# First loads without w_in beside them, q read straight from its turn, w_out with four rows a partition, and a new order of work

## Chip, cores and metric

One core of one Trainium2 chip. The metric is the time of one execution on the device in microseconds; lower is better. Times of the kernel before are a median of three runs, beside one execution taken with the hardware profiler.

## What is computed

Gated linear attention over 4 batches, 8 heads, 768 steps and a head width of 48, and behind it a two-layer perceptron on its output.

```python
f = 1.0 / (1.0 + np.exp(-f_logit))
for t in range(S):
    state = f[:, :, t, :, None] * state + np.einsum('bhd,bhe->bhde', k[:, :, t], v[:, :, t])
    y[:, :, t] = np.einsum('bhd,bhde->bhe', q[:, :, t], state)
...
x = attn_out.transpose(0, 2, 1, 3).reshape(B * S, H * D)     # 3072 x 384
h = x @ w_in                                                 # w_in 384 x 2048
g = np.maximum(0.01 * h, h)
return g @ w_out                                             # w_out 2048 x 384
```

## The kernel before

**Units.** The sequence is cut into 6 chunks of 128 steps; a chunk of one batch is a *unit* (24 of them, unit u = 4 * chunk + batch), and two units make a pair m = u // 2 for the perceptron. For a unit, `gate_exp`, `gate_ln`, `gate_pe` and `decay_*` turn f_logit into running decays, `k_scale` and `q_scale` multiply k and q by them, `turn_pe` transposes both, `score_pe` and `mask` make the causal scores, `mix_pe` the output y, `state_pe`, `state_dve` and `state_pool` the running state, and `y_out`, `x_pe`, `x_out` bring y as x (transposed) into `xTs`. Late units use DMA transposes (`turn_dma`, `x_dma`) instead.

**The perceptron.** `up(m, g, bank)` makes 2 of the 16 blocks of 128 hidden columns for a pair (six matmuls of 256 columns, weights from `w_in_b`), `up_act(m, g, bank)` applies the leaky ReLU into `gTs`, and `down(u, half, bank)` sums 8 hidden blocks for a unit (eight matmuls of 384 columns, `w_out_b` streaming). `put` and `out_dma` store the result.

**The first quad.** Units 0 to 3 (the first chunk of all four batches) are treated together by the functions with q_ ahead of their names: time is interleaved over the partitions (partition 4 t + b holds steps 4 t to 4 t + 3 of batch b), the gates are four pairs of accumulating matmul groups (`q_gate_pe`), the scaled k and q are transposed (`q_turn_pe`) and copied out of PSUM with the columns sorted by batch (`q_turn_out`), so that the scores of one batch read contiguous columns.

**Queues.** Every engine works through its own instructions in program order, and the order is written out by hand as the long list of calls at the end of the kernel (`manual_schedule`). SP issues all loads of f, k, q and v and all stores; ACT issues four of the first twelve loads (L77 to L89); POOL issues the six loads of weights, which convert float32 to bfloat16 on the way (`load_w_in`, two halves of 1,024 columns; `load_w_out`, four groups). A load on SP or ACT waits until the load eight before it has landed. PSUM has eight banks of 2 KB a partition, and the last argument of most calls names one. `idle_pe(n, bank)` issues n matmuls on zeros.

**The start.** SP and ACT issue f, k and q of the quad; POOL builds the small constant tiles and then issues both halves of w_in, as its first loads. ACT computes exp and ln of the gates, PE runs 40 filler matmuls and then the gate matmuls, and DVE and POOL scale k, then q.

## Time and profile before

| | us |
|---|---|
| median of 3 runs (192.94 to 193.77) | 193.02 |
| the profiled execution | 192.63 |
| its span, first to last instruction | 190.8 |
| mean granted TensorE clock of it | 0.982 of full speed |

The page gives busy times of the engines, the chain of waits that ended last, and the costliest groups of instructions by line. PE is the matmul engine, PEld its weight loads, which overlap with PE; DVE, ACT and POOL are the vector, scalar and general engines, SP the one that only issues transfers. A name with a q behind it (SPq, POOLq) is that engine's sequencer. In the DMA views, q0 is the queue of POOL's loads, q1 that of SP and q10 that of ACT; a share is the time that the queue's packets took, of 16 engines, and shares of queues can add up to more than 100%. The two instructions most of the time goes to:

```profile
L412 PE MATMUL ps<-xT,w_in_b 128*128 128x256 bf16 x576 | 70.6, 273 | 0.0
L422 PE MATMUL ps<-w_out_b,gT 128*128 128x384 bf16 x384 | 68.4, 326 | 0.0
```

L412 is the matmul of `up`, L422 that of `down`. The mean duration of one (273 and 326 ns) is longer than the step between two of them, since matmuls are pipelined.

### The profile page before, as it was taken

The page shows a single profiled execution, that of the slowest core. Times are in us where ns is not written, and L with a number is a line of the kernel's source. Part 1 is how long each engine was busy: PE and PEld are TensorE (multiplying, and loading weights), DVE is VectorE, ACT ScalarE, POOL GpSimd, SP SyncE. Part 2 cuts the span into 40 slices and gives each one's busy share as a digit, 9 for nine tenths or more (in the row PEclk, how much of TensorE's full clock was granted, in tenths as well). Part 3 has the DMA queues.
Part 4 walks back from the last instruction along what each step waited for, and adds up shares of the span by engine and source line. Part 5 has one row for each costly group of instructions (what it writes and reads, how often), then busy time and mean ns, then how long its engine had stood idle before and what let it go on. Part 6 is the DMA issues. An engine that isn't in the chain of part 4 may idle for free.

```text
span 190.8 us, 4830 instructions
## 1 busy us (share of the span) xinstructions
PE 175.7 (92%) x1905; PEld 136.3 (71%) x1905; DVE 87.4 (46%) x193; ACT 124.1 (65%) x266; POOL 59.2 (31%) x109
## 2 busy tenths in 40 slices
PE   4952679999999999999999999999999999999992
PEld 2841459886679778768877787877668787776861
DVE  7001799313597557547556436894528304010000
ACT  2661176994479879967968778986458665642822
POOL 8000855620143644441532512844502500000000
PEclk9997599999999999999999999999999999999999
DMA  4999899999088989899999999972742490113202
GB/s 143 264 222 259 172 190 213 166 185 178 25 196 190 212 176 235 167 228 200 217 193 192 221 195 191 227 157 65 156 115 62 79 138 0 45 43 83 82 3 84
DMA packets 106679, 29.42 MB, mean 154 GB/s; under 512 B 97696, under 2 KB 105888, under 8 KB 106656
## 3 DMA queue, kind: packets, MB, share of 16 engines
q1 hardware_dynamic: 102656, 25.18, 62.2%
q0 software_dynamic: 2912, 3.15, 10.1%
q10 hardware_dynamic: 1088, 0.79, 1.3%
q8 instruction: 15, 0.25, 0.5%
q14 instruction: 8, 0.07, 0.1%
HBM read 25.17 MB, written 4.72 MB: 157 GB/s over the span
## 4 chain that ended last, share of the span: by engine, by line
PE 84%; DMA 9%; ACT 2%; SPq 1%; DVE 1%; issue 1%; POOL 1%; POOLq 0%; ACTq 0%
PE ps L412 33%; PE ps L422 33%; DMA qq<-in_q_dram 6%; PE ps L332 3%; PE ps L357 3%; DMA fq<-in_f_logit_dram 2%; PE ps L371 2%; PE ps L368 2%; PE ps L304 2%; PE ps L379 2%; PE ps L402 2%; SPq L69 1%; PE ps L139 1%; PE ps L223 1%; ACT kqh L145 1%
## 5 line engine op out<-in xcount | busy, mean ns | idle before, releaser
L412 PE MATMUL ps<-xT,w_in_b 128*128 128x256 bf16 x576 | 70.6, 273 | 0.0
L422 PE MATMUL ps<-w_out_b,gT 128*128 128x384 bf16 x384 | 68.4, 326 | 0.0
L417 ACT ACTIVATE gT<-ps 128x512 bf16<-128x512 f32 x96 | 56.8, 604 | 12.3 <-PE ps L412 10.2
L412 PEld LDWEIGHTS <-w_in_b 128*128 128x128 bf16 x576 | 54.3, 98 | 7.7
L422 PEld LDWEIGHTS <-gT 128*128 128x128 bf16 x384 | 36.2, 98 | 20.6
L361 DVE TENSOR_TENSOR wm<-ps,ut 128x512 bf16<-128x512 f32 x40 | 24.9, 682 | 14.7 <-ACT gT L417 10.4
L288 POOL CAST sb<-sf 64x192 bf16<-64x192 f32 x40 | 15.1, 378 | 35.9 <-PE ps L368 31.3
L145 ACT COPY osb<-ps 128x384 f32<-128x384 f32 x23 | 11.0, 480 | 20.7 <-PE ps L422 20.7
L319 DVE TENSOR_TENSOR kqh<-k_raw,em_t 128x384 bf16<-128x384 f32 x14 | 7.9, 567 | 12.9 <-ACT em_t L311 12.7
L323 POOL TENSOR_TENSOR kqh<-q_raw,a_t 128x384 bf16<-128x384 f32 x11 | 10.3, 938 | 10.4 <-issue 7.1
L393 POOL TENSOR_TENSOR sf<-sf,a_end 128x192 f32<-128x192 f32 x16 | 9.2, 576 | 13.1 <-DVE sf L388 12.6
L147 DVE CAST xn<-ps 128x384 bf16<-128x384 f32 x12 | 6.5, 554 | 12.6 <-ACT osb L145 7.8
L311 ACT ACTIVATE em_t<-ps 128x384 bf16<-128x384 f32 x20 | 9.8, 497 | 2.5 <-PE ps L307 2.5
L147 DVE COPY kqT<-ps 128x512 bf16<-128x512 bf16 x17 | 6.8, 421 | 8.6 <-PE ps L332 5.3
L298 ACT ACTIVATE lf<-f_raw 128x384 bf16<-128x384 f32 x20 | 10.5, 532 | 0.1
L145 ACT COPY kqT<-ps 128x512 bf16<-128x512 bf16 x11 | 6.3, 587 | 6.6 <-PE ps L332 3.8
L295 ACT ACTIVATE f_raw<-f_raw 128x384 f32<-128x384 f32 x20 | 10.4, 526 | 0.0
L139 PE MATMUL ps<-fill 128*128 128x256 bf16 x60 | 9.2, 317 | 1.1 <-DVE ind L129 1.1
L314 ACT ACTIVATE a_t<-ps 128x384 bf16<-128x384 f32 x20 | 9.9, 508 | 0.0
L145 ACT CAST xn<-ps 128x384 bf16<-128x384 f32 x12 | 5.8, 480 | 4.7 <-PE ps L371 2.9
L387 DVE TENSOR_TENSOR sf<-sf,ps 64x192 f32<-64x192 f32 x16 | 5.5, 342 | 7.1 <-PE ps L379 4.2
L139 PEld LDWEIGHTS <-fill 128*128 128x128 bf16 x60 | 6.7, 114 | 2.8 <-issue 1.3
(88 smaller groups left out, 194.1 us busy)
## 6 DMA issues: line engine op xcount, KB each, us to landing
v_raw<-in_v_dram SPq DMA_DIRECT2D x24, 192.0 KB, 4.0
out_dram<-osb SPq DMA_DIRECT2D x24, 192.0 KB, 2.5
f_raw<-in_f_logit_dram SPq DMA_DIRECT2D x20, 192.0 KB, 3.9
k_raw<-in_k_dram SPq DMA_DIRECT2D x20, 192.0 KB, 4.0
q_raw<-in_q_dram SPq DMA_DIRECT2D x20, 192.0 KB, 4.0
w_in_b<-in_moe_w_in_dram POOLq DMA_DIRECT2D x2, 768.0 KB, 12.2
w_out_b<-in_moe_w_out_dram POOLq DMA_DIRECT2D x4, 384.0 KB, 8.6
qq<-in_q_dram SPq DMA_DIRECT2D x4, 192.0 KB, 12.1
```

Source lines behind the costliest of these rows:

```text
L139: nc.tensor.matmul(bank(bk)[:, 0:256], fill[:, 0:128], fill[:, 0:256], start=True, stop=True)
L145: eng.copy(out=out, in_=in_)
L147: eng.tensor_copy(out=out, in_=in_)
L288: nc.gpsimd.tensor_copy(out=state_b[b][r, :, e * D:(e + 1) * D], in_=state_f[b][r])
L295: nc.scalar.activation(raw[u]["f"], raw[u]["f"], AF.Exp, scale=-1.0)
L298: nc.scalar.activation(lfs[u % R_LF][:, :, 0:D], raw[u]["f"], AF.Ln, bias=1.0)
L314: nc.scalar.activation(a_ts[u % R_EM], bank(bk)[:, 0:H * D], AF.Exp, scale=-1.0)
L323: eng.tensor_mul(qhs[u % R_KQS][:, :, 0:D], r["q"], a_ts[u % R_EM])
L361: nc.vector.tensor_mul(wms[e][u % R_WM], bank(bk).rearrange("p (i n) -> p i n", i=P2), ut[:, None, :].to_broadcast([128, P2, 128]))
L412: nc.tensor.matmul(bank(bk)[:, i * 256:(i + 1) * 256], w_in_b[:, kk, ff * 128:(ff + 1) * 128], xTs[m % R_XT][:, kk].rearrange("p a n -> p ...
L417: nc.scalar.activation(gTs[m % GBUFS][:, 2 * g:2 * g + 2].rearrange("p f a n -> p (f a n)"), bank(bk), AF.Prelu, alpha=0.01)
L422: nc.tensor.matmul(bank(bk)[:, 0:KD], gTs[u // 2 % GBUFS][:, ff, u % 2, :], w_out_b[:, ff, :], start=(ff == 0), stop=(ff == NF - 1))
```

## The change

- **Loads of the quad.** All four k loads are issued by SP; ACT issues only two of f and loads its table of functions right after.
- **w_in.** Both halves move from POOL's first work to behind `q_q_scale(G, 0, 1)`, a new one-column copy from q (`touch('q')`) and `q_k_scale(G, 1, 0)`. The copy reads q of all four batches, so it waits for the four q loads.
- **q straight.** `q_q_out` copies the turned q out of PSUM as it lies (512 contiguous columns); `q_score_pe` picks one batch's columns with a step of four elements as it streams them. k is sorted by batch as before.
- **w_out.** Partition p of group g holds rows 512 g + 4 p to 512 g + 4 p + 3, so each partition's part is one piece of 6,144 bytes of the source. For the sums to match, hidden block ff = 4 g + i of `up` is now made of the columns 512 g + 4 n + i of w_in (n = 0 to 127): the weight load reads w_in_b with a step of four elements (`w_in_p`). The first half of w_in still holds ff 0 to 7, so `up(m, g)` with g from 0 to 3 needs the first half alone.
- **Order.** The list of calls is a new one. It has the same calls of `up`, `down`, `score_pe`, `mix_pe`, `state_pe`, `turn_pe`, `x_pe`, `turn_dma` and `x_dma`; 52 filler matmuls instead of 60; and some copies and products on another engine (ACT has 18 `y_out` instead of 12, and 24 `put` instead of 23). Of the list, the diff below shows the new lines up to the second store, without the old ones.

```diff
@@ -79,11 +79,11 @@
     first_load(nc.sync, "f", 1)
     first_load(nc.scalar, "f", 3)
     first_load(nc.sync, "k", 0)
-    first_load(nc.scalar, "k", 2)
+    nc.scalar.preload_act_table_set("natural_log_exp_and_others")
     first_load(nc.sync, "k", 1)
-    first_load(nc.scalar, "k", 3)
+    first_load(nc.sync, "k", 2)
+    first_load(nc.sync, "k", 3)
     first_load(nc.sync, "q", 0)
-    nc.scalar.preload_act_table_set("natural_log_exp_and_others")
     first_load(nc.sync, "q", 1)
     first_load(nc.sync, "q", 2)
     first_load(nc.sync, "q", 3)
@@ -102,6 +102,7 @@
     nc.gpsimd.memset(ones_col, 1.0)
 
     w_in_b = const.tile([128, NK, FF], BF16, tag="w_in")
+    w_in_p = w_in_b.rearrange("p a (g n i) -> p a g n i", n=128, i=4)
     w_out_b = const.tile([128, NF, KD], BF16, tag="w_out")
 
     fill = const.tile([128, 512], BF16, tag="fill")
@@ -170,6 +171,13 @@
         for name, src in (("f", f_logit), ("k", k), ("q", q), ("v", v)):
             load_part(u, name, src)
 
+    seen = const.tile([128, 1], FP32, tag="seen")
+
+    def touch(what):
+        src = {"f": fq[:, 0, 0, 0:1], "k": kq[:, 0, 0, 0:1], "q": qq[:, 0, 0, 0:1],
+               "v": raws["v_raw"][1][:, 0, 0:1], "w": raws["v_raw"][3][:, 0, 0:1]}[what]
+        nc.gpsimd.tensor_copy(out=seen, in_=src)
+
     def load_w_in(g):
         w = FF // 2
         nc.gpsimd.dma_start(out=w_in_b[:, :, g * w:(g + 1) * w],
@@ -178,7 +186,7 @@
     def load_w_out(g):
         w = NF // 4
         nc.gpsimd.dma_start(out=w_out_b[:, g * w:(g + 1) * w, :],
-                            in_=moe_w_out.rearrange("(a p) n -> p a n", p=128)[:, g * w:(g + 1) * w, :])
+                            in_=moe_w_out.rearrange("(g p i) n -> p g i n", p=128, i=w)[:, g, :, :])
 
     st = {u: {} for u in range(NU)}
 
@@ -186,7 +194,7 @@
     emq = [const.tile([128, 4, 4, D], BF16, name=f"emq{i}", tag=f"emq{i}") for i in range(2)]
     aq = [const.tile([128, 4, 4, D], BF16, name=f"aq{i}", tag=f"aq{i}") for i in range(2)]
     kTq = [const.tile([128, 2, 4, 128], BF16, name=f"kTq{i}", tag=f"kTq{i}") for i in range(2)]
-    qTq = [const.tile([128, 2, 4, 128], BF16, name=f"qTq{i}", tag=f"qTq{i}") for i in range(2)]
+    qTq = [const.tile([128, 2, 512], BF16, name=f"qTq{i}", tag=f"qTq{i}") for i in range(2)]
     wmq = [[[wms[e][2 * hh + bp] for bp in range(2)] for e in range(2)] for hh in range(2)]
     a_endq = const.tile([128, P2, B], FP32, tag="a_endq")
 
@@ -222,23 +230,21 @@
             for pp in range(2):
                 nc.tensor.transpose(tp[:, pp, j, :], src[hh][:, j, 2 * pp:2 * pp + 2, :], ident)
 
-    def q_turn_out(dst, hh, bk, pp):
+    def q_k_out(eng, hh, pp, bk):
         tp = bank16(bk).rearrange("p (a j t b) -> p a b t j", a=2, j=4, b=4)
-        return dict(out=dst[hh][:, pp].rearrange("p b (t j) -> p b t j", j=4), in_=tp[:, pp])
-
-    def q_k_out(eng, hh, pp, bk):
-        move(eng, **q_turn_out(kTq, hh, bk, pp))
+        move(eng, kTq[hh][:, pp].rearrange("p b (t j) -> p b t j", j=4), tp[:, pp])
 
     def q_q_out(eng, hh, pp, bk):
-        move(eng, **q_turn_out(qTq, hh, bk, pp))
+        move(eng, qTq[hh][:, pp], bank16(bk).rearrange("p (a n) -> p a n", a=2)[:, pp])
 
     def q_score_pe(hh, bp, bk0, bk1):
-        pw = [bank(bk).rearrange("p (b a n) -> p b a n", b=2, a=2) for bk in (bk0, bk1)]
-        for bl in range(2):
+        for b in (2 * bp, 2 * bp + 1):
             for pp in range(2):
                 for e in range(2):
-                    nc.tensor.matmul(pw[e][:, bl, pp, :], kTq[hh][64 * e:64 * e + 64, pp, 2 * bp + bl, :],
-                                     qTq[hh][64 * e:64 * e + 64, pp, 2 * bp + bl, :], start=True, stop=True)
+                    r = slice(64 * e, 64 * e + 64)
+                    i = 2 * (b % 2) + pp
+                    nc.tensor.matmul(bank((bk0, bk1)[e])[:, i * 128:(i + 1) * 128], kTq[hh][r, pp, b, :],
+                                     qTq[hh][r, pp].rearrange("p (j t b) -> p b t j", j=4, b=4)[:, b], start=True, stop=True)
 
     def q_wf_act(hh, bp, e, bk):
         nc.scalar.copy(out=wmq[hh][e][bp], in_=bank(bk).rearrange("p (i n) -> p i n", i=4))
@@ -409,7 +415,7 @@
         for i in range(2):
             for kk in range(NK):
                 ff = 2 * g + i
-                nc.tensor.matmul(bank(bk)[:, i * 256:(i + 1) * 256], w_in_b[:, kk, ff * 128:(ff + 1) * 128],
+                nc.tensor.matmul(bank(bk)[:, i * 256:(i + 1) * 256], w_in_p[:, kk, ff // 4, :, ff % 4],
                                  xTs[m % R_XT][:, kk].rearrange("p a n -> p (a n)"),
                                  start=(kk == 0), stop=(kk == NK - 1))
 
...
     q_exp_act(0)
     q_exp_act(1)
     q_ln_act(0)
     q_ln_act(1)
     load_part(0, "v", v)
+    idle_pe(40, 7)
+    q_gate_pe(0, 1, 0)
+    load_part(1, "v", v)
+    q_gate_pe(0, 0, 1)
+    load_part(3, "v", v)
+    q_decay_act(0, 1, emq, 1.0, 0)
+    q_gate_pe(1, 0, 2)
+    q_decay_act(0, 1, aq, -1.0, 0)
+    load_part(2, "v", v)
+    q_k_scale(V, 0, 1)
+    q_decay_act(0, 0, emq, 1.0, 1)
+    q_gate_pe(1, 1, 3)
+    q_q_scale(G, 0, 1)
+    q_decay_act(0, 0, aq, -1.0, 1)
+    load_part(4, "f", f_logit)
+    q_k_scale(V, 0, 0)
+    q_decay_act(1, 0, emq, 1.0, 2)
+    q_end_pe(4)
+    q_decay_act(1, 0, aq, -1.0, 2)
+    q_q_scale(V, 0, 0)
+    load_part(4, "k", k)
+    touch('q')
+    q_decay_act(1, 1, emq, 1.0, 3)
+    q_k_scale(G, 1, 0)
+    q_turn_pe(khq, 0, 0, 5)
+    q_q_scale(V, 1, 0)
+    q_end_act(4)
+    q_decay_act(1, 1, aq, -1.0, 3)
+    q_turn_pe(khq, 0, 1, 5)
+    load_part(4, "q", q)
+    q_turn_pe(qhq, 0, 0, 6)
+    q_k_scale(V, 1, 1)
     load_w_in(0)
+    q_k_out(A, 0, 1, 5)
+    q_turn_pe(qhq, 0, 1, 6)
+    cast_v(V, 1)
+    q_turn_pe(khq, 1, 0, 7)
+    q_k_out(A, 0, 0, 5)
+    load_part(4, "v", v)
+    q_turn_pe(qhq, 1, 0, 0)
+    q_q_scale(V, 1, 1)
     load_w_in(1)
     q_turn_pe(khq, 1, 1, 7)
+    q_q_out(A, 0, 1, 6)
+    q_q_out(V, 0, 0, 6)
+    cast_v(G, 3)
+    q_k_out(A, 1, 1, 7)
+    q_k_out(V, 1, 0, 7)
+    idle_pe(3, 3)
     q_turn_pe(qhq, 1, 1, 0)
+    cast_v(G, 0)
+    q_score_pe(0, 0, 1, 2)
+    q_q_out(A, 1, 1, 0)
+    q_q_out(V, 1, 0, 0)
+    cast_v(G, 2)
+    q_score_pe(0, 1, 4, 3)
+    q_mask(0, 0, 0, 1)
+    q_back_pe(2, 5)
+    q_back_pe(0, 6)
+    q_wf_act(0, 1, 1, 3)
+    q_score_pe(1, 0, 7, 0)
+    q_mask(0, 0, 1, 2)
+    q_back_out(A, 2, 5)
+    q_back_pe(1, 1)
     q_mask_pool(0, 1, 1)
+    q_back_pe(3, 3)
+    q_mask(1, 0, 1, 0)
+    q_back_out(A, 0, 6)
+    q_score_pe(1, 1, 2, 5)
+    load_part(5, "f", f_logit)
+    q_back_out(A, 3, 3)
+    q_mask(1, 0, 0, 7)
+    state_pe(2, 0)
+    q_wf_act(1, 1, 1, 5)
+    state_pe(0, 6)
+    q_mask(1, 1, 0, 2)
+    q_back_out(A, 1, 1)
+    state_pe(3, 3)
     q_mix_pe(1, 7)
+    q_mask_pool(1, 1, 1)
+    q_mask(0, 1, 0, 4)
+    q_mix_pe(0, 5)
+    y_out(A, 1, 7)
+    y_out(V, 0, 5)
+    state_pe(1, 2)
     q_state_dve(0)
+    x_pe(1, 1)
+    q_mix_pe(3, 4)
+    q_mix_pe(2, 7)
+    x_out(A, 1, 1)
+    q_state_dve(2)
     x_pe(0, 5)
+    q_state_pool(0)
+    y_out(A, 3, 4)
+    y_out(A, 2, 7)
+    x_out(V, 0, 5)
+    q_state_pool(2)
+    q_state_dve(3)
+    gate_exp(4)
+    idle_pe(6, 6)
+    x_pe(3, 6)
+    up(0, 2, 1)
+    gate_ln(4)
+    x_out(V, 3, 6)
+    q_state_pool(3)
     q_state_dve(1)
+    x_pe(2, 0)
+    up(0, 0, 4)
+    load_part(5, "k", k)
+    up_act(0, 2, 1)
+    x_out(V, 2, 0)
     q_state_pool(1)
+    up(0, 3, 5)
+    up_act(0, 0, 4)
+    load_part(5, "q", q)
+    up(0, 5, 7)
+    load_w_out(0)
+    up_act(0, 3, 5)
+    load_part(5, "v", v)
+    up(1, 5, 3)
     load_w_out(1)
+    up_act(0, 5, 7)
+    up(0, 4, 6)
     load_w_out(3)
+    up_act(1, 5, 3)
+    up(0, 6, 2)
     load_w_out(2)
+    up_act(0, 4, 6)
+    up(0, 7, 1)
+    up_act(0, 6, 2)
+    gate_pe(4, 0)
+    up(0, 1, 4)
+    up_act(0, 7, 1)
+    load_part(6, "f", f_logit)
+    decay_em(4, 0)
+    cast_v(V, 4)
     up(1, 7, 5)
+    decay_a(4, 0)
+    k_scale(V, 4)
+    up(1, 3, 7)
+    up_act(0, 1, 4)
+    q_scale(G, 4)
+    up_act(1, 7, 5)
+    up(1, 2, 3)
+    up_act(1, 3, 7)
+    state_pe(4, 6)
+    up(1, 1, 2)
+    up_act(1, 2, 3)
+    state_dve(4)
+    turn_pe(4, 1)
+    up_act(1, 1, 2)
     up(1, 6, 0)
+    turn_k(V, 4, 1)
+    gate_exp(5)
+    turn_q(V, 4, 1)
+    down(1, 0, 4)
+    gate_ln(5)
     up_act(1, 6, 0)
+    down(0, 0, 5)
     load_part(6, "k", k)
+    gate_pe(5, 7)
     load_part(6, "q", q)
+    up(1, 0, 3)
+    decay_em(5, 7)
+    decay_a(5, 7)
+    down(1, 1, 4)
+    load_part(6, "v", v)
+    up_act(1, 0, 3)
+    load_part(7, "f", f_logit)
+    down(0, 1, 5)
+    put(A, 1, 4)
     k_scale(V, 5)
+    load_part(7, "k", k)
+    down(3, 0, 6)
     q_scale(V, 5)
+    put(A, 0, 5)
+    out_dma(1)
+    cast_v(V, 5)
+    turn_pe(5, 2)
+    out_dma(0)
...
```

More of the change, by code (lines that the diff above doesn't have):

```diff
@@ L643 @@
+    load_part(8, "f", f_logit)
+    up_act(1, 4, 7)
+    gate_pe(6, 0)
+    load_part(8, "k", k)
+    mask(4, 0, 3)
+    cast_v(G, 6)
+    decay_em(6, 0)
+    down(3, 1, 6)
+    load_part(8, "q", q)
+    decay_a(6, 0)
+    mask(4, 1, 4)
+    k_scale(G, 6)
+    gate_exp(7)
+    mask(5, 0, 5)
+    load_part(8, "v", v)
+    gate_ln(7)
+    down(2, 1, 1)
+    q_scale(G, 6)
+    mask(5, 1, 2)
+    put(A, 3, 6)
+    load_part(9, "f", f_logit)
+    mix_pe(4, 7)
+    put(A, 2, 1)
     mix_pe(5, 3)
-    decay_em(6, 5)
@@ L663 @@
[L663 to L683 removed]
+    x_pe(5, 6)
+    x_out(A, 4, 5)
+    load_part(9, "k", k)
+    gate_pe(7, 2)
@@ new lines @@
+    down(8, 0, 6)
+    state_pool(11)
+    y_out(A, 11, 7)
+    decay_a(13, 5)
+    load_part(19, "v", v)
+    decay_em(13, 5)
+    q_scale(V, 13)
+    x_pe(11, 2)
+    k_scale(G, 13)
+    down(9, 1, 1)
+    load_part(20, "f", f_logit)
+    x_out(A, 11, 2)
+    load_part(19, "k", k)
+    gate_pe(14, 0)
+    turn_pe(13, 3)
+    put(A, 9, 1)
+    decay_em(14, 0)
+    up(5, 1, 4)
+    load_part(19, "q", q)
+    turn_k(V, 13, 3)
+    decay_a(14, 0)
+    k_scale(G, 14)
+    turn_q(V, 13, 3)
+    up(5, 2, 7)
@@ new lines @@
+    gate_ln(20)
+    mask(17, 1, 3)
+    up(7, 6, 2)
+    up_act(7, 3, 1)
+    up_act(7, 7, 5)
+    mix_pe(16, 4)
+    up_act(7, 6, 2)
+    state_pe(18, 6)
+    mix_pe(17, 0)
+    state_pool(16)
+    y_out(V, 16, 4)
+    gate_ln(21)
+    gate_pe(20, 1)
+    down(14, 0, 3)
+    state_dve(18)
+    x_dma(16)
+    y_out(A, 17, 0)
+    decay_em(20, 1)
+    x_dma(17)
+    state_pool(17)
+    decay_a(20, 1)
+    k_scale(V, 20)
+    decay_a(18, 7)
+    down(15, 0, 5)
+    q_scale(V, 20)
+    q_scale(G, 18)
```

1295 lines of the change are left out of this document (531 added, 764 removed).

## The prediction

> **What bounds the kernel now.** I read the page's head first (who is busy), then the chain of waits in order of time, then the engines by stage.
>
> ```profile
> span 190.8 us, 4830 instructions
> PE 175.7 (92%) x1905; PEld 136.3 (71%) x1905; DVE 87.4 (46%) x193; ACT 124.1 (65%) x266; POOL 59.2 (31%) x109
> ```
> ```profile
> 7.25 12.03 DMA qq<-in_q_dram
> ...
> 20.69 1.24 POOL khq L211
> ...
> 31.44 1.31 PE ps L412 x12
> 32.75 0.20 PE ps L257 x8
> 32.95 0.17 PE ps L402 x3
> 33.12 0.17 PE ps L379 x4
> ...
> 34.77 3.93 PE ps L412 x36
> ...
> 187.39 0.48 ACT osb L145
> ```
> ```profile
> 18.10:31.44 13.34, 9.46 (x136) 7.77 (x137) 10.97 (x20) 5.76 (x12) 7.87 (x10) 0.78 0.98 195
> 31.44:187.39 155.95, 155.87 (x1674) 120.06 (x1672) 72.03 (x151) 109.71 (x239) 47.35 (x85) 1.00 0.71 144
> ```
>
> The chain columns are start, length, what. The windows show length, then busy time of PE, weight loads, DVE, ACT and POOL, the granted clock, the DMA share and GB/s. From the first `up` (31.44) to the last matmul (187.39) PE is busy 155.87 of 155.95 us at full clock: that stretch is nothing but matmuls. So a gain can come only from an earlier first `up`, a loss also from new holes or slower matmuls in that stretch. Before 31.44 the chain stands for 12.03 us on the last q load. What delays q:
>
> ```profile
> DMA packets 3393, 3.23 MB, mean 246 GB/s; under 512 B 577, under 2 KB 2625, under 8 KB 3393
> ## 3 DMA queue, kind: packets, MB, share of 16 engines
> q0 software_dynamic: 800, 1.57, 64.9%
> q1 hardware_dynamic: 1986, 1.22, 34.0%
> q10 hardware_dynamic: 607, 0.43, 10.3%
> ```
> ```profile
> L175 POOL DMA_DIRECT2D w_in_b<-in_moe_w_in_dram x2: 778/856/933, 3.1 to 4.0; - x2
> ...
> DMA to landing us min/median/max: 10.2/12.2/14.1
> ```
>
> The first is the DMA view of 5.0 to 18.1 us: w_in (queue q0) holds 64.9% of the engines while k and q (q1, q10) trickle. The tile view of w_in gives its two issues, at 3.1 and 4.0, landing at 3.1 + 10.2 = 13.3 and 4.0 + 14.1 = 18.1. q lands one microsecond later, at 7.25 + 12.03 = 19.28.
>
> **The change part by part.** *q without w_in.* w_in now sits in POOL's program behind a `q_scale` (which itself needs q), the `touch`, and a `k_scale`. f, k and q are 12 loads of 196,608 bytes, 2.36 MB.
>
> ```profile
> DMA packets 1032, 0.75 MB, mean 251 GB/s; under 512 B 53, under 2 KB 1032, under 8 KB 1032
> ```
> ```profile
> DMA packets 1515, 1.20 MB, mean 299 GB/s; under 512 B 86, under 2 KB 1438, under 8 KB 1515
> ```
> ```profile
> SPq L69 <- DMA fq<-in_f_logit_dram: 1.5, 1, 1.5
> ```
>
> By 5.0 us 0.75 MB had moved (view of 2 to 5 us). The other 1.61 MB take 5.4 us at 299 GB/s (4 to 8 us) or 6.5 us at the 246 of 5 to 18.1: q lands at 10.4 to 11.5, against 19.28. SP's two extra k issues cost nothing: SP waited 1.5 us there for the first f load's landing. ACT's earlier table load also hides under its wait for f.
>
> *When the weights come.* The rows for POOL and ACT:
>
> ```profile
> 10.49 0.48 ACT L206 ACTIVATE aq<-ps 128x384 bf16<-128x384 f32 x1
> ...
> 12.72 0.56 ACT L206 ACTIVATE aq<-ps 128x384 bf16<-128x384 f32 x1
> ```
> ```profile
> 3.03 0.10 POOL L102 MEMSET ones_col<- 128x1 bf16 x1
> ...
> 19.45 1.28 POOL L211 TENSOR_TENSOR qhq<-qq,aq 128x384 bf16<-128x384 f32 x1 [14.68 <-DMA v_raw<-in_v_dram]
> 20.69 2.10 POOL L211 TENSOR_TENSOR khq<-kq,emq 128x384 bf16<-128x384 f32 x2
> 22.74 0.92 POOL L211 TENSOR_TENSOR qhq<-qq,aq 128x384 bf16<-128x384 f32 x1
> 26.93 0.64 POOL L147 CAST v_b<-v_raw 128x384 bf16<-128x384 f32 x1
> ```
>
> The first `aq` is ready at 10.97, so POOL starts `q_scale` at 11.0 to 11.5, ends it 1.28 later, does the touch (no row; between the one-column memset's 0.10 and the 128x384 cast's 0.64; I take 0.2, one column being nearer the memset), then `k_scale` in 1.05 (half of 2.10): w_in is issued at about 13.8. Behind it on POOL wait three v casts and a mask, not needed before about 17.
>
> From issue to both halves landed it took 18.1 - 3.1 = 15.0 us before, beside 1.65 MB on the hardware queues. Its first 15 packets stand in 6 to 7 us, 3 us after the issue, none before:
>
> ```profile
> q0 software_dynamic: 15, 0.03, 20.7%
> ```
>
> Bounds: w_in occupied the engines 0.649 x 13.1 = 8.5 us. Alone it lands at 13.8 + 3 + 8.5 = 25.3; at half of the engines at 13.8 + 3 + 17 = 33.8. Its company will be 192-byte rows of v and of unit 4, which w_out met before:
>
> ```profile
> ## 3 DMA queue, kind: packets, MB, share of 16 engines
> q0 software_dynamic: 1983, 1.49, 85.2%
> q1 hardware_dynamic: 3380, 0.64, 36.4%
> ```
>
> In 33 to 45 us the weights kept 85.2%. By that share it lands at 26.8, by its own old pace at 13.8 + 15.0 = 28.8. I take 28.0, within these.
>
> *First `up`.* The first half of w_in, about 22.5, is enough for three `up` calls; the fourth, up(0,5), needs the second. Will the attention stage be ready? Before, the last `q_scale` ended at 22.74 + 0.92 = 23.66 and the first `up` came 7.8 us later. Now the last `aq` ends near 13.5 (13.28 plus a 128x16 activation moved ahead), and DVE's chain of seven operations from 10.7 ends at 14.5 (0.55 each) to 16.7 (0.87, what this row gives beside POOL):
>
> ```profile
> 19.40 1.74 DVE L211 TENSOR_TENSOR qhq<-qq,aq 128x384 bf16<-128x384 f32 x2 [4.35 <-DMA qq<-in_q_dram]
> ```
>
> I take 15.6; 15.6 + 7.8 = 23.4, and two more mixes now stand ahead: first `up` at 24. Six matmuls cost 3.93/6 = 0.655 us, so three `up` calls and one x_pe take 2.14; PE reaches up(0,5) at 26.1 and **waits some 1.9 us for w_in**, until 28.0. In work done, that equals a first `up` at 28.0 - 2.14 = 25.9, 5.5 us earlier.
>
> *q straight from PSUM, masks, engine swaps, 52 instead of 60 filler matmuls* all lie before up(0,5), where weights now end last: worth nothing while w_in binds. If that cover goes they decide whether 24 is 23 or 25. The scores now read q at a step of four elements; not in the trace. Bounds: nothing, or double the 0.87/16 = 0.054 us of each of 32 matmuls, 1.7 us, still inside the 1.9. I take nothing: a matmul that is longer there is covered by the same wait.
>
> ```profile
> 23.39 0.87 PE L240 MATMUL ps<-qTq,kTq 64*128 64x128 bf16 x16
> ```
>
> *Four rows a partition.* w_out's transfers have larger pieces (6,144 bytes read) and a quarter of the packets. Between nothing and w_in's occupancy (8.5 us for 1.57 MB against w_out's 0.852 x 12 = 10.2), 2 us of engine time are saved. They queue behind w_in, at 28.0 to about 39; the first `down` comes 11 `up` calls later, 28.0 + 7.2 + 1.0 = 36.2, and starts with groups issued first. Meanwhile unit 4 and 5 loads get little bandwidth (0.64 MB in 12 us above). I charge 0.2.
>
> The price is that each `up` weight load now reads every fourth column, 576 times. No strided weight load stands in the trace. Nearest rows:
>
> ```profile
> 14.82 0.51 PEld L264 LDWEIGHTS <-lfq 128*128 128x128 bf16 x16
> ```
> ```profile
> 22.48 0.69 DVE L147 COPY qTq<-ps 128x512 bf16<-128x512 bf16 x1 [0.73 <-ACT qTq L145]
> ```
> ```profile
> L147 DVE COPY kqT<-ps 128x512 bf16<-128x512 bf16 x17 | 6.8, 421 | 8.6 <-PE ps L332 5.3
> ```
>
> Packed loads follow each other in about (0.51 - 0.10)/15 = 27 ns; an `up` matmul lasts 109 ns (3.93/36). A DVE copy with that step is 690 ns against 421, 1.64 times; 27 x 1.64 = 44 ns stays under 109. Bounds: 0, and the other end without limit in the trace: each ns above 109 costs 0.58 us. I take 0 because 109 leaves a factor of four.
>
> [...]
>
> *Order made anew.* The same 96 up, 48 down, 20 mix and state calls follow. After the first `up`, before had a mix, two x_pe and a state (0.71 by the chain's rows); now one x_pe and three fillers (0.17 + 0.33): -0.2. PE had 0.08 us of holes, so a new order can only add: 0 to 3 us; I take 0.2.
>
> Sum on the profiled execution (192.63, that is 190.8 and 1.83 around it): -5.5 - 0.2 + 0.2 + 0.2 = -5.3, 187.3. The median of the runs is 0.39 above that execution: **187.7**.
>
> **The rivals.**
> - *w_in lands before PE asks for it* (by 26.1): the attention stage binds, first `up` at 24, gain 7.4 less 0.2: 185.8. For it: 85.2% in like company. Against: 28.8 at its old pace.
> - *w_in late*: each microsecond after 28.0 costs one. At 30 to 33, 189.7 to 192.7; at half share, 33.8, 193.5 and nothing is won. Against: no window shows w_in below 64.9%.
> - *Strided weight loads slower than their matmul* (the slower side): at `up`, from 118 ns a load on, (118 - 109) x 0.576 = 5.2, the gain is gone; at twice the matmul's 109 it costs 63 us, 250 in all. Against: the factor of four.
> - *Holes in the long stretch*: unit 4 to 9 loads come late behind both weights, or the new order fits worse. At 3 to 7 us of holes, 190.7 to 194.7. For it:
>
> ```profile
> 20.00:25.00 5.00, 3.96 (x46) 3.12 (x47) 4.03 (x6) 2.09 (x4) 3.93 (x5) 0.61 0.98 189
> ```
>
> the clock fell to 0.61 after PE's pause for q, so sparse work can cost twice. Against: before, no hole stood in PE after 31.44, although w_out ran there.
>
> **How the numbers follow.** Forecast (186 to 190) 0.54; earlier weights 0.12; late weights 0.14; strided loads 0.08; holes 0.12. 0.5% of 193.02 is 0.97, about what a measurement of this kernel can tell from no change: faster is below 192.05, slower above 193.99. Faster: 0.54 + 0.12 + 0.11 (late) + 0.04 (holes) = 0.81, which I lower to 0.78 for the unseen order. Same 0.07. Slower 0.15. The range 185.0 to 192.6 leaves out the strided case, the end of the late one and half the holes, about 0.2.
>
> **What would show it.** Right: q landed by 11.5; w_in issued near 14 and landed 27 to 29; a wait of PE at up(0,5); 36 `up` matmuls in a row still 3.93 us; the stretch after it without holes. Wrong: `up` matmuls slower than 109 ns; up(0,5) not waiting, or past 31; PE idle by more than 1 us in total after 30.

## The result, and the profile after

The kernel after takes 191.18 us (median of 5 runs, 190.90 to 191.87), the kernel before 193.09 beside it: a ratio of 0.9905, 95% interval 0.9877 to 0.9933. It is faster by 1.9 us, where 5.3 had been forecast. The profiled execution took 191.70, that is 0.93 less than the one of before (192.63). Here and below a median is over all runs, while a ratio and its interval leave out runs more than 1.5% above the fastest of their kernel.

From the page's head, then the DMA view of 5 to 11.8 us (its last columns are KB each and the median time to landing), then the chain of waits in order of time, from 7 us to 29 (start, length, what):

```profile
span 189.8 us, 4822 instructions
PE 177.3 (93%) x1897; PEld 142.3 (75%) x1897; DVE 81.7 (43%) x181; ACT 128.8 (68%) x276; POOL 58.2 (31%) x112
```
```profile
qq<-in_q_dram SPq DMA_DIRECT2D x4, 192.0 KB, 4.1
```
```profile
7.02 0.61 SPq L69
...
12.99 0.52 POOL seen L179
13.51 1.19 POOL khq L219
14.69 0.89 POOL w_in_b L183
15.58 12.54 DMA w_in_b<-in_moe_w_in_dram
28.12 0.05 issue
28.16 0.74 PE ps L418 x5
```

The step that cost 12.03 us for q is gone: the fourth q load is issued by 7.0 and lands 4.1 later, at about 11.1. In its place stand 12.54 us of w_in's second half, issued at 15.58 and landed at 28.12. Now the instructions of PE, with the wait before each and what ended it:

```profile
16.08 1.95 PE L246 MATMUL ps<-qTq,kTq 64*128 64x128 bf16 x16
...
25.65 0.27 PE L418 MATMUL ps<-xT,w_in_b 128*128 128x256 bf16 x1 [0.18 <-DVE xT L148]
28.16 0.74 PE L418 MATMUL ps<-xT,w_in_b 128*128 128x256 bf16 x5 [2.25 <-DMA w_in_b<-in_moe_w_in_dram]
```
```profile
54.97 0.49 PE L140 MATMUL ps<-fill 128*128 128x256 bf16 x3 [1.03 <-DVE sf L394]
```
```profile
156.09 1.59 PE L418 MATMUL ps<-xT,w_in_b 128*128 128x256 bf16 x13 [0.99 <-DMA xT<-xn]
```

The first `up` has one matmul at 25.65 and then stops: the second waits until the second half of w_in has landed, though `up(0,2)` multiplies columns of the first half alone, which had landed at 23.7 (issued at 14.6, 9.1 to landing). Behind that stand two new holes: three filler matmuls that wait for bank 4 (1.03 us), and `up(10,5)`, whose x comes by a DMA transpose that hasn't landed (0.99). The long stretch, by windows (length, then busy PE, weight loads, DVE, ACT, POOL, granted clock, DMA share, GB/s), and the end of the chain:

```profile
28.16:186.46 158.30, 156.19 (x1661) 126.40 (x1661) 64.37 (x133) 112.24 (x245) 44.58 (x81) 1.00 0.69 147
```
```profile
171.38 3.93 PE ps L418 x36
```

This accounts for the whole difference. The stretch of matmuls starts at 28.16 and not at 31.44: -3.28. PE is idle in it for 158.30 - 156.19 = 2.11 us and not 0.08: +2.03. PE's busy time in it is 156.19 and not 155.87: +0.32. The sum is -0.93, which is what the two executions differ by. 36 `up` matmuls still take 3.93 us, so the stepped weight loads stay hidden, though each has become longer, 114 ns on average where it was 98 before, as the row of the costliest groups shows (busy, mean ns of one):

```profile
L418 PEld LDWEIGHTS <-w_in_b 128*128 128x128 bf16 x576 | 61.0, 114 | 5.4 <-DMA w_in_b<-in_moe_w_in_dram 2.8
```

### The profile page after: what moved, and what is told of

It is laid out like the page before. It is cut to its first block, busy times and chain, and to the rows that moved or that the text cites. A ratio compares the mean times of both kernels' runs of the same rounds, so it can differ in the third digit from the quotient of the medians.

```text
span 189.8 us, 4822 instructions
## 1 busy us (share of the span) xinstructions
PE 177.3 (93%) x1897; PEld 142.3 (75%) x1897; DVE 81.7 (43%) x181; ACT 128.8 (68%) x276; POOL 58.2 (31%) x112
## 4 chain that ended last, share of the span: by engine, by line
PE 79%; DMA 11%; SPq 3%; POOL 1%; ACT 1%; issue 1%; DVE 0%; ACTq 0%; POOLq 0%
PE ps L428 33%; PE ps L418 32%; DMA w_in_b<-in_moe_w_in_dram 7%; SPq L69 3%; PE ps L338 3%; PE ps L363 3%; DMA xT<-xn 2%; DMA v_raw<-in_v_dram 2%; PE ps L377 2%; PE ps L310 2%; PE ps L374 2%; PE ps L385 1%; PE ps L408 1%; POOL khq L219 1%; PE ps L313 1%
## 5 line engine op out<-in xcount | busy, mean ns | idle before, releaser
L418 PEld LDWEIGHTS <-w_in_b 128*128 128x128 bf16 x576 | 61.0, 114 | 5.4 <-DMA w_in_b<-in_moe_w_in_dram 2.8
L146 ACT COPY osb<-ps 128x384 f32<-128x384 f32 x24 | 11.5, 479 | 21.8 <-PE ps L428 21.6
L294 POOL CAST sb<-sf 64x192 bf16<-64x192 f32 x40 | 14.1, 353 | 28.7 <-PE ps L374 25.5
L329 POOL TENSOR_TENSOR kqh<-q_raw,a_t 128x384 bf16<-128x384 f32 x12 | 11.2, 931 | 20.4 <-issue 12.9
L325 POOL TENSOR_TENSOR kqh<-k_raw,em_t 128x384 bf16<-128x384 f32 x7 | 6.4, 918 | 23.1 <-ACT em_t L317 9.1
L146 ACT CAST xn<-ps 128x384 bf16<-128x384 f32 x18 | 8.2, 485 | 3.3 <-PE ps L377 3.0
L148 POOL CAST v_b<-v_raw 128x384 bf16<-128x384 f32 x13 | 7.3, 582 | 9.1 <-DMA v_raw<-in_v_dram 9.0
L140 PE MATMUL ps<-fill 128*128 128x256 bf16 x52 | 7.6, 308 | 2.2 <-DVE ind L130 1.1
L399 POOL TENSOR_TENSOR sf<-sf,a_end 128x192 f32<-128x192 f32 x16 | 8.4, 524 | 1.1 <-DVE sf L394 0.4
L338 PE MATMUL ps<-ident,kqh 128*128 128x128 bf16 x112 | 8.5, 219 | 0.0
(87 smaller groups left out, 187.8 us busy)
## 6 DMA issues: line engine op xcount, KB each, us to landing
w_in_b<-in_moe_w_in_dram POOLq DMA_DIRECT2D x2, 768.0 KB, 10.8
```

Of the source, the lines that this page charges most:

```text
L146: eng.copy(out=out, in_=in_)
L148: eng.tensor_copy(out=out, in_=in_)
L294: nc.gpsimd.tensor_copy(out=state_b[b][r, :, e * D:(e + 1) * D], in_=state_f[b][r])
L325: eng.tensor_mul(khs[u % R_KQS][:, :, 0:D], raw[u]["k"], em_ts[u % R_EM])
L329: eng.tensor_mul(qhs[u % R_KQS][:, :, 0:D], r["q"], a_ts[u % R_EM])
L338: nc.tensor.transpose(tp[:, i, p, :], src[:, 2 * p:2 * p + 2, :], ident)
```

## The experiments

All ratios stand against runs of the kernel before on the same chip. The rows come from at least four chips, so ratios compare better than medians. Where the profile of an experiment is told, it is one execution of it. old_q and probe, which the table leaves out, ran once each.

| run | what it is | median us | ratio (95% interval) |
|---|---|---|---|
| after | the change | 191.18 | 0.9905 (0.9877 to 0.9933) |
| two_tiles | after, w_in in two tiles | 191.27 | 0.9846 (0.9779 to 0.9914) |
| old_weights | after, both weights as before | 195.56 | 0.999 (0.9951 to 1.0029) |
| old_q_timed | after, q sorted by batch | 191.94 | 0.9878 (0.9835 to 0.9921) |
| touch_k | after, w_in held back for k alone | 193.26 | 0.9991 (0.9971 to 1.001) |
| before_late | before, w_in late and nothing else | 187.75 | 0.972 (0.9687 to 0.9752) |
| late_step_q | before_late and the stepped q | 188.69 | 0.9759 (0.973 to 0.9787) |
| late_four | before_late and the new weights | 188.78 | 0.976 (0.9714 to 0.9806) |
| no_holes | after, edited at its two holes | 189.63 | 0.9822 (0.9786 to 0.9858) |
| two_no_holes | no_holes, w_in in two tiles | 188.87 | 0.9758 (0.9724 to 0.9792) |
| two_no_holes_old_q | that, q sorted by batch | 187.42 | 0.9679 (0.9642 to 0.9715) |
| four_first | that, two `up` calls swapped | 186.83 | 0.9671 (0.9641 to 0.9701) |

### Undoing one part of the change

**two_tiles.** A tile for each half of w_in:

```diff
-    w_in_b = const.tile([128, NK, FF], BF16, tag="w_in")
+    w_in_h = [const.tile([128, NK, FF // 2], BF16, name=f"w_in{i}", tag=f"w_in{i}") for i in range(2)]
```

> The changed kernel with w_in in two tiles, one for each half, and nothing else. Theory 1 (the wait for the second half is a matter of the one tile: the second matmul of up(0,2) waits for a load that it does not read): the first three up calls run from about 25.7 us on, the wait stands at up(0,5), at most 0.5 us long, and the time falls by 1.8 to 2.2 us against 191.18, to about 189.2. Rival (the weights bind whatever the tiles are, or another load is what is waited for): the six matmuls of up(0,2) still start at 28.2 and the time stays within 0.5 us.

By medians nothing was won (191.27, against 191.18 for the kernel after); by the ratios it is 1.1 us ((0.9905 - 0.9846) x 193), with intervals that overlap. The wait at the second matmul is gone. These are the PE rows of the first `up` and of the first `down`, then the window of 20 to 25 us, first of two_tiles and then of the kernel after:

```profile
27.39 0.81 PE L418 MATMUL ps<-xT,w_in 128*128 128x256 bf16 x6 [0.18 <-DVE xT L148]
```
```profile
42.56 0.65 PE L428 MATMUL ps<-w_out_b,gT 128*128 128x384 bf16 x3 [1.25 <-DMA w_out_b<-in_moe_w_out_dram]
```
```profile
20.00:25.00 5.00, 5.00 (x58) 3.43 (x56) 2.61 (x5) 2.97 (x6) 2.22 (x2) 0.50 1.10 189
20.00:25.00 5.00, 4.72 (x72) 3.60 (x71) 3.87 (x9) 3.27 (x8) 1.87 (x4) 0.72 1.12 196
```

All six matmuls run, but x is ready only at 27.4, 1.7 us later than in the profile of the kernel after: between 20 and 25 us PE is busy all the time at half clock, where the clock was 0.72 there. So in this execution a late attention stage takes the place of most of the wait for the second half; and the first `down` then waited 1.25 us for w_out.

**old_weights.** Packed columns of w_in, one row of w_out a partition:

```diff
-    w_in_p[:, kk, ff // 4, :, ff % 4]
+    w_in_b[:, kk, ff * 128:(ff + 1) * 128]
...
-    in_=moe_w_out.rearrange("(g p i) n -> p g i n", p=128, i=w)[:, g, :, :]
+    in_=moe_w_out.rearrange("(a p) n -> p a n", p=128)[:, g * w:(g + 1) * w, :]
```

> The changed kernel with the weight pattern of before: w_in read in packed columns, w_out one row a partition. Theory 1 (weight loads with a step hide under their matmul): steps of up matmuls stay at 109 ns, the time changes by less than 0.5 us. Rival (the step costs time, seen in weight loads of 114 ns on average after against 98 before): up matmuls get faster and the time falls by 1 us or more.

The expectation, a change of less than 0.5 us, was missed: by the ratios the time is 1.6 us longer than that of the kernel after, and not by the weight loads. The profiled execution took 195.50, in runs of 192.27 to 196.87. The group of w_in's loads is back at 98 ns, the first `up` runs all its six matmuls, and the new row is a wait of PE for w_out:

```profile
L418 PEld LDWEIGHTS <-w_in_b 128*128 128x128 bf16 x576 | 54.4, 98 | 8.6 <-issue 1.5
```
```profile
26.96 0.81 PE L418 MATMUL ps<-xT,w_in_b 128*128 128x256 bf16 x6 [0.18 <-DVE xT L148]
```
```profile
44.23 1.98 PE L428 MATMUL ps<-w_out_b,gT 128*128 128x384 bf16 x7 [3.37 <-DMA w_out_b<-in_moe_w_out_dram]
```

The second half of w_in landed at 27.4 there (issued at 14.8, 12.6 to landing), after the second matmul: with packed columns, in the same order of work and in one tile, that matmul didn't wait for it. w_out took up to 12.7 us from issue to landing, up to 10.8 in the kernel after, and was issued from 29.2 on and not from 27.9. So in this execution the old pattern doesn't bring w_out in time; in before_late, below, it does. Part of the wait is the later issue: two_tiles, with four rows a partition and an issue from 29.6 on, waited 1.25 us at the same place.

**old_q, old_q_timed.** q sorted by batch as it leaves PSUM, as before:

```diff
-        move(eng, qTq[hh][:, pp], bank16(bk).rearrange("p (a n) -> p a n", a=2)[:, pp])
+        tp = bank16(bk).rearrange("p (a j t b) -> p a b t j", a=2, j=4, b=4)
+        move(eng, qTq[hh][:, pp].rearrange("p b (t j) -> p b t j", j=4), tp[:, pp])
```

> The changed kernel with q sorted by batch as it leaves PSUM, as before. Theory (the step of four elements makes the score matmuls of the first quad slow: 16 in 1.95 us and 8 in 1.05 after, against 8 in 0.40 before): 8 of them take 0.40 to 0.65 us again, the attention stage is ready 0.5 to 1.5 us sooner, and the time stays the same, since w_in still ends last at 28.1. Rival (the clock, not the step, made them slow): they stay above 1.0 us for 8.

> The kernel after with q sorted by batch as before, this time timed in rounds. Theory: 1.1 to 1.7 us less than the kernel after, 189.5 to 190.1 (one run gave 189.8). Rival (w_in's second half, which the second up matmul waits for, covers the scores): 190.8 to 191.4.

The single execution of old_q took 189.83, with 16 scores in 0.62 us and groups of 8 in 0.40, as its expectation had it; they had taken 1.95 and 1.05. In the ten runs of old_q_timed the median was 191.94, with four at 189.7 to 190.1 (mean granted clock 1.00) and six at 191.9 to 192.6 (0.98 to 0.99): no gain that can be told from the kernel after. The median lies in neither of the two ranges expected, though four of the runs lie in the theory's. The execution profiled in old_q_timed is one of the longer ones:

```profile
23.66 0.27 PE L419 MATMUL ps<-xT,w_in_b 128*128 128x256 bf16 x1 [0.18 <-DVE xT L148]
27.47 1.25 PE L419 MATMUL ps<-xT,w_in_b 128*128 128x256 bf16 x5 [3.54 <-DMA w_in_b<-in_moe_w_in_dram]
```
```profile
25.00:30.00 5.00, 2.53 (x14) 1.88 (x15) 1.23 (x4) 0.60 (x1) 2.85 (x6) 0.68 1.15 204
```

x is ready two microseconds earlier than in the kernel after (23.66 against 25.65), and most of that goes into a longer wait at the second matmul. After 3.54 us of waiting, five matmuls take 1.25 us and not 0.74: the granted clock is 0.50 from 26.8 to 30.3 us, 0.68 over the window shown, where old_q's execution, after a wait of 1.61, has 1.00.

**touch_k.** w_in waits for k and is issued ahead of the first `q_scale`:

```diff
+    touch('k')
+    load_w_in(0)
+    load_w_in(1)
     q_q_scale(G, 0, 1)
...
-    touch('q')
```

> The changed kernel with w_in held back until k has landed (not q), and issued ahead of POOL's q_scale. Theory (some 2.5 us pass between the issue and the first packets, so a wait for k lets q through as well and brings both halves 4 to 5 us earlier): q lands by 12.2, w_in by 24.5, the first up starts at 25.7 with the attention stage, the time falls by 2.0 to 2.5 us. Rival (w_in then takes the engines from v and unit 4's loads): v lands late, the attention stage is ready 1 us or more later, less than 1 us is won.

Nothing was won over the kernel before. POOL's rows show who paid:

```profile
9.66 1.73 POOL L183 DMA_DIRECT2D w_in_b<-in_moe_w_in_dram  x2 [0.35 <-issue]
11.65 1.28 POOL L219 TENSOR_TENSOR qhq<-qq,aq 128x384 bf16<-128x384 f32 x1 [0.26 <-DMA qq<-in_q_dram]
12.90 1.22 POOL L219 TENSOR_TENSOR khq<-kq,emq 128x384 bf16<-128x384 f32 x1
22.76 1.40 POOL L148 CAST v_b<-v_raw 128x384 bf16<-128x384 f32 x3 [8.64 <-DMA v_raw<-in_v_dram]
```

q is in time, but now v, the load behind it, comes under w_in, and POOL waits 8.64 us for it. In the kernel after, these casts start at 16.4 and not at 22.76: holding w_in back for q protects v too. The rival of the expectation came true.

### One part of the change alone

**before_late.** The kernel before with w_in issued late:

```diff
-    load_w_in(0)
...
-    load_w_in(1)
...
     q_q_scale(G, 0, 0)
+    nc.gpsimd.tensor_copy(out=seen, in_=qq[:, 0, 0, 0:1])
...
     q_k_scale(G, 1, 0)
+    load_w_in(0)
+    load_w_in(1)
```

> The kernel before with one edit: both halves of w_in are issued behind the one-column copy of q and one k_scale, as in the change; weights pattern, q and order stay. Theory (the late weights give the start 3.3 us, the new order then loses 2.1 in two holes): first up at about 28, the stretch behind it as smooth as before, the time lower by 2.5 to 3.5 us, 189.6 to 190.6, under the changed kernel. Rival (holes come with the earlier start, whatever the order, because loads of units 4 and on come later): holes of 2 us or more behind the first up, 191 or above.

187.75, a ratio of 0.972, below the 189.6 to 190.6 expected: this edit alone gives what was forecast for the whole change. PE's rows of the first two `up` calls, of its profile:

```profile
25.89 0.82 PE L414 MATMUL ps<-xT,w_in_b 128*128 128x256 bf16 x6
27.03 0.72 PE L414 MATMUL ps<-xT,w_in_b 128*128 128x256 bf16 x5 [0.32 <-DMA w_in_b<-in_moe_w_in_dram]
```

Here, with packed columns in one tile, `up(0,0)` runs to its end on the first half, and the second call, `up(0,7)`, which does read the second half, waits 0.32 us for it. Behind it PE waits for nothing longer than 0.3 us, and for w_out, with one row a partition, not at all.

**late_step_q, late_four.** before_late with one more part of the change each:

```diff
+        move(eng, qTq[hh][:, pp], bank16(bk).rearrange("p (a n) -> p a n", a=2)[:, pp])
...
+    qTq[hh][64 * e:64 * e + 64, pp].rearrange("p (j t b) -> p b t j", j=4, b=4)[:, 2 * bp + bl]
```
```diff
+    w_in_p[:, kk, ff // 4, :, ff % 4]
...
+    in_=moe_w_out.rearrange("(g p i) n -> p g i n", p=128, i=w)[:, g, :, :]
```

> before_late (187.75: the kernel before with only w_in issued late) plus the turned q left in its stepped form, all else in the old order. Theory (the stepped q is what eats part of the gain): in the run after, 16 scores took 1.95 us against 0.87, and a moving operand at a step of four elements took 116 ns a matmul against 58 at full clock in the run probe; 32 scores cost 1.1 to 1.7 us more ahead of the first up, which moves from 25.9 to 27.0 or later: 188.9 to 189.5. Rival (the forecast's: w_in lands last, at 26.9, and covers the longer scores): no more than 0.3, 187.6 to 188.1.

> before_late plus the four-rows-a-partition w_out and the stepped w_in columns that go with it, all else in the old order. Theory: the stepped weight loads lie under their matmuls (33 ns a load against 109 of the matmul), the up step stays 109 to 110 ns; w_out lands some 1 us earlier, which nothing waits for in the old order: 187.4 to 188.1. Rival (the stepped weights take back part of the gain): 96 up calls at 113 ns and more, 190 or later.

Each gives back about a microsecond by medians; the intervals of both still touch before_late's. The first 16 scores, in before_late and then in late_step_q, and late_step_q's first `up`:

```profile
17.24 0.62 PE L242 MATMUL ps<-qTq,kTq 64*128 64x128 bf16 x16
```
```profile
16.93 1.95 PE L242 MATMUL ps<-qTq,kTq 64*128 64x128 bf16 x16
...
26.95 1.25 PE L414 MATMUL ps<-xT,w_in_b 128*128 128x256 bf16 x10
```

1.95 us in place of 0.62, and the first `up` 1.06 later than in before_late, with no matmul that waits for w_in. The forecast's cover did not hold: this stage, and no longer w_in, set the time. All 32 scores took 4.05 us (1.95, 1.05 and 1.05), against 1.63 (0.62, 0.61 and 0.40): 2.4 us more, of which 1.06 reach the first `up`.

From the starts of the records, the scores of before_late and late_step_q come in pairs, one on each half of the rows, 3 to 4 ns apart, and a pair follows the last after 56 ns packed at full clock and after 224 with the step. So the step costs four times here, and not two. The 224 ns stand alike at a clock of 1.00 and of 0.50.

In late_four the scores are as before, but:

```profile
25.86 0.27 PE L415 MATMUL ps<-xT,w_in_b 128*128 128x256 bf16 x1
27.87 1.39 PE L415 MATMUL ps<-xT,w_in_b 128*128 128x256 bf16 x11 [1.73 <-DMA w_in_b<-in_moe_w_in_dram]
```

Against before_late only the weights' pattern differs, and the second matmul waits for the second half again. So it is the stepped columns in one tile that tie the first `up` to both halves; the kernel after and old_weights say the same in the new order. (Of the four runs two lie at 189.4, the profiled one among them, and two at 187.8 and 188.2, where 187.4 to 188.1 was expected. Whether the wait was as long in those two no profile shows.)

### The price of a step of four, by itself

**probe.** The kernel after with 256 more matmuls behind its last store, on the constant tile `fill`, so its time is longer by that work. Groups of 32, with weights or moving operand packed or read at a step of two or four elements:

```diff
+    for weights, moving in ((flat, fill[:, 0:4]), (by2, fill[:, 0:4]), (by4, fill[:, 0:4]),
+                            (flat, flat), (flat, by2), (flat, by4),
+                            (flat, fill[:, 0:256]), (by4, fill[:, 0:256])):
+        for _ in range(32):
+            nc.tensor.matmul(bank(5)[:, 0:n], weights, moving, start=True, stop=True)
```

> The changed kernel with eight groups of 32 matmuls on zeros behind its last work, no computation left out; the whole is longer by the added groups. From the trace: the step between matmuls of 4 columns with packed weights, with weights at a step of 2 and of 4 elements (27 ns if the step is free; 27 to 54 if it halves the rate; 109 or more if it could slow up); the step between matmuls of 128 columns streamed packed, at a step of 2 and of 4 (56 ns if free, 110 to 130 if the scores were slow by the step); and 256 columns with packed and with stepped weights (109 both if hidden).

From the starts of the records, the step between two matmuls of a group: with 4 columns, where the weight load sets it, 25 ns packed, 25 at a step of two, 33 at a step of four. With 128 columns at full clock, 58 ns for a moving operand at a step of two, 116 at a step of four; packed it was 55. With 256 columns, 109 ns with packed weights and 109 with weights at a step of four. Two windows of one microsecond, one at a step of two and one at a step of four, and one of three microseconds between the groups:

```profile
193.25:194.25 1.00, 1.00 (x20) 1.00 (x19) 0.00 (x0) 0.00 (x0) 0.00 (x0) 1.00 0.00 0
195.00:196.00 1.00, 1.00 (x11) 1.00 (x10) 0.00 (x0) 0.00 (x0) 0.00 (x0) 1.00 0.00 0
190.00:193.00 3.00, 3.00 (x31) 3.00 (x29) 0.00 (x0) 0.00 (x0) 0.00 (x0) 0.50 0.03 5
```

20 matmuls in a microsecond against 11 (those that reach into the window from its edges are counted in). In these matmuls a step of four halves the rate at which a moving operand is read; a weight load takes a third longer, and 33 ns vanish under 109. The last row belongs to the section on the hardware.

### Putting the parts right together

**no_holes.** The kernel after without the three fillers on bank 4, and with two `up` calls of pair 9 ahead of `up(10,5)`:

```diff
-    idle_pe(3, 4)
     up(2, 3, 1)
...
+    up(9, 5, 0)
+    up_act(9, 2, 5)
+    up(9, 7, 3)
+    up_act(9, 5, 0)
     up(10, 5, 6)
-    up_act(9, 2, 5)
+    up_act(9, 7, 3)
```

> The changed kernel without the three fillers ahead of up(2,3), which wait for a bank, and with up(9,5) and up(9,7) moved ahead of up(10,5), which waits for a DMA transpose. Theory (both holes are matters of the order): the 1.03 us hole falls to 0.7 or less and the fillers' 0.33 us go, the 1.15 us hole goes; the time falls by 1.3 to 2.0 us against 191.18. Rival (what is late there makes the next work late too): the holes turn up at the next call, less than 0.5 us is won.

189.63, a ratio of 0.9822, and by the ratios 0.0083 x 193 = 1.6 us less than the kernel after. PE's rows at the two places:

```profile
53.48 1.25 PE L418 MATMUL ps<-xT,w_in_b 128*128 128x256 bf16 x10 [0.69 <-ACT xT L146]
```
```profile
150.64 5.62 PE L418 MATMUL ps<-xT,w_in_b 128*128 128x256 bf16 x50
```

The second hole is gone. Of the first, 0.69 is left: without the fillers `up(2,3)` itself stands there and waits for its x.

**two_no_holes_old_q, then two_no_holes and four_first.** The edits of two_tiles, no_holes and old_q together; the same without the sorted q; and the first with two calls exchanged:

```diff
-    up(0, 5, 7)
+    up(0, 1, 7)
...
-    up(0, 1, 4)
+    up(0, 5, 4)
```

> The kernel after with w_in in two tiles, without the two holes of the new order (the fillers on bank 4; up(10,5) ahead of its transfer) and with q sorted by batch as before. Theory (the account is complete: 1.1 to 1.7 us by the stepped q, 2.0 by the two holes, up to 1 by the wait of the second matmul for w_in's second half): 191.2 less 3.4 to 4.2, 187.0 to 187.8. Rival (the new order costs something else besides): 188.7 or later, with the first up no later than 25.5.

> The kernel after with w_in in two tiles and without the two holes of the new order, the turned q left stepped. It stands between no_holes (189.63) and two_no_holes_old_q (187.42), which differ in both. Theory A (the second matmul's wait for w_in's second half is the greater part): 187.6 to 188.4, with three up calls done before the second half lands. Theory B (the stepped q is the greater part: with it the attention stage ends as late as w_in lands, so two tiles win nothing): 189.2 to 189.9, with the first up at 26 or later.

> two_no_holes_old_q (187.42) with up(0,1), which needs w_in's first half alone, in the place of up(0,5), which needs the second, and the other way round. Theory (up(0,5) waits there for the second half, as the forecast had it): one up call more, 0.65 us, is done within that wait: 186.7 to 187.0. Rival (the wait is not for the second half, or a later one takes its place): 187.3 to 187.6.

187.42, 188.87 and 186.83. two_no_holes lies between the two theories' figures. By the ratios the sorted q is worth (0.9758 - 0.9679) x 193 = 1.5 us there, with intervals that don't meet, and two tiles (0.9822 - 0.9758) x 193 = 1.2 us over no_holes, with intervals that overlap; in both profiles the first `up` ends at 27.8. So beside the stepped q the worth of two tiles is not settled. PE's rows of the start, first of two_no_holes_old_q, then of four_first:

```profile
24.13 0.81 PE L419 MATMUL ps<-xT,w_in 128*128 128x256 bf16 x6 [0.18 <-DVE xT L148]
24.78 0.33 PE L409 MATMUL ps<-ident,xn 128*128 128x128 bf16 x3
24.95 1.47 PE L419 MATMUL ps<-xT,w_in 128*128 128x256 bf16 x12
27.90 2.27 PE L419 MATMUL ps<-xT,w_in 128*128 128x256 bf16 x19 [1.48 <-DMA w_in<-in_moe_w_in_dram]
```
```profile
24.37 0.82 PE L419 MATMUL ps<-xT,w_in 128*128 128x256 bf16 x6 [0.18 <-DVE xT L148]
25.02 0.33 PE L409 MATMUL ps<-ident,xn 128*128 128x128 bf16 x3
25.19 4.75 PE L419 MATMUL ps<-xT,w_in 128*128 128x256 bf16 x42
```

The first is the start that the prediction described: x at 24, three `up` calls and an x_pe on the first half, then a wait at `up(0,5)`, until 27.9. In the second, `up(0,1)` stands in that place, and 42 matmuls follow each other without a wait. The medians differ by 0.59 us, a little less than one `up` call (0.655); the two intervals overlap widely, so the size of this last step isn't settled. four_first is the fastest of all that ran, 4.4 us below the kernel after and 6.4 below before by medians.

## Why the prediction was right and wrong

**What bounds the kernel, and what q costs: right.** q lands at 11.1 (forecast 10.4 to 11.5), and before_late alone, at a ratio of 0.972, gives 5.4 us. That this is so near the -5.5 forecast for the start is partly luck: in the old order the attention stage sets the first `up` (25.89) and not the weights, whose second half lands at 26.9 and not 28.

**When the weights come: right in the sum, by two errors that cancel.** They were issued at 14.6 and not 13.8, of which 0.3 is the touch (0.52 us, where 0.2 had been taken). The first packets came 2.1 us behind the issue and not 3, so at 16.7 where 16.8 had been taken. The second half landed at 28.12, forecast 28.0; the first half at 23.7 and not 22.5, which cost nothing, since x came later still. touch_k shows what an earlier issue does: v pays (POOL waits 8.64 us for it).

**First `up`: here the prediction failed.** The step was "The first half of w_in, about 22.5, is enough for three `up` calls". In the kernel after it is enough for one matmul, so the 2.14 us of work that were to be done before the second half landed were done after it: -3.28 us and not -5.5. late_four against before_late shows that the stepped columns in one tile bring this wait, and two_no_holes_old_q, with two tiles, shows the three calls running as forecast. In the kernel after, old_q_timed and late_four alike the matmul that runs reads row block kk = 0 of w_in, and the one that waits reads kk = 1. Why the second matmul is tied to a transfer that writes other columns (how the dependency on a stepped slice of one tile is worked out) no run shows.

**The scores: mis-sized, and in the kernel after hidden.** "I take nothing" stood between 0 and 1.7 us for a q read at a step of four, and even the upper end was too low: the step costs the pairs of scores four times their time (224 ns against 56), 2.4 us on 32 scores. In the kernel after, x was ready at 25.65 and not 24, and the wait for w_in covered that, for the wrong reason: PE was waiting at its second `up` matmul already. With q sorted x is ready at 23.7 to 24.7 in four kernels, so 24 itself was right. Where the wait is taken away the step shows: 1.06 us at the first `up` in late_step_q, 1.5 us between two_no_holes and two_no_holes_old_q. So two_tiles and old_q_timed, which each undo one of the two, win little (1.1 and 0.5 us by the ratios, neither clear of noise): each uncovers the other. That a step could at most double a matmul was the author's estimate; the probe shows just that for a moving operand of all 128 rows (116 ns for 128 columns, against 55 packed), the pairs of scores twice as much.

**Four rows a partition: right in its price.** The weight loads grew from 98 to 114 ns in the records and stayed hidden, 36 `up` matmuls at 3.93 us; one by itself takes 33 ns, where 44 had been estimated. w_out caused no wait in the kernel after; with the old pattern PE waited 3.37 us for it in old_weights. In four_first, whose first `down` comes at 38.75, it was 0.46 with the new pattern. In the old order four rows are not needed: before_late has the old pattern and no such wait. That stepped reads of a single tile would tie both halves together was no term of the forecast.

**Order made anew: the second step that failed.** "a new order can only add: 0 to 3 us; I take 0.2" was right in its bounds and wrong in its value: 2.03 us of holes. no_holes takes out the one at 155 us and a third of the one at 54.

**The sum.** Forecast -5.3, measured -0.93 on the profiled executions. The 4.4 between them are 2.2 at the start (-3.28 for -5.5), 1.8 in holes (2.03 for 0.2), and 0.3 for the rest: PE was busy by 0.32 us more where 0.2 less had been expected (0.52), less w_out's charge of 0.2, which didn't fall due.

**The rivals.** *Holes in the long stretch* came true in kind, at 2.0 us and not 3 to 7. *w_in late* fell (28.12), *strided weight loads* fell. *w_in lands before PE asks for it* is nearly what four_first became. The clock that fell to 0.61, told there as a matter of PE's pause, also falls without one; the last section has the rows.

**What stays open.** The moment at which w_in's second half lands lies between 26.6 and 28.2 in the profiles of the kernel after and its relatives (touch_k, which issues it earlier, apart); no run tells what decides it. old_q_timed falls into two groups of runs 2 us apart, at a mean clock of 1.00 and of 0.98 to 0.99. In the one profiled, of the slower group, 3.4 us at half clock stand right at the start of the long stretch, which would cost up to 1.7 us of matmuls (an estimate from 0.50 x 3.4); in old_q's execution, at 189.83, there is no such stretch. What decides whether it comes is open too.

## What to carry to other kernels

Holding a large transfer back until all the small ones that the start needs first have landed brought q 8.2 us earlier in the kernel after, and made before_late 5.4 us faster. Held back for part of them only, as in touch_k, it won nothing. Try this edit alone before a new order is built around it. A partial wait (half of a tile) has to be looked up in the trace or given a tile of its own, above all where the reads are stepped. When undoing either of two parts wins little, undo both: each may be hiding the other.
